# Moving three output-weight blocks of a small MLP to three narrow transfers, and its side table to 128 rows

## The chip, the cores and the metric

One core of a Trainium2 chip runs the whole kernel. The metric is device time in microseconds (us), the median of several executions; for the kernel before it is 706.14 us in 3 runs (705.8 to 706.69).

## What is computed

A decode step of one token for 8 sequences: `x` (8 x 512) is normalised, goes through grouped-query attention over a cache of 4096 positions (8 key/value heads of 128, 32 query heads), and beside that through a gated MLP; the attention output is scaled by the SiLU of the MLP's output and added to `x`. All data is float32.

```
xn = layernorm(x)
q  = xn @ wq ; o = softmax(q k^T / sqrt(128)) v ; s = o @ wo
z  = gelu(xn @ w_in)                 # 8 x 1792
z1, z2 = z[:896], layernorm(z[896:])
y  = (z1 * (w_sp * z2 + b_sp)) @ w_out   # w_out: 896 x 512
out = x + s * silu(y)
```

The key and value caches are 134 MB each, `wq` and `wo` 8.4 MB each, `w_in` 3.7 MB, `w_out` 1.8 MB: seven blocks of 128 rows by 512 columns, 256 KB each.

## The kernel before

**Loads.** A ring of three slots (`slot()`, 128 x 16384 floats, 8 MB each) takes all big loads, issued by SyncE in program order: the MLP weights (`w_mlp`, L64), `wq` (L78), then for each of 8 heads two halves of K (`load_k`, L302) and two of V (`load_v`, L309), at last `wo` in seven pieces (L326). A load into a slot that was used before waits, on SyncE, until the last reader of the slot is done; what stands behind it in SyncE's queue waits too. The fourth load, K's second half of head 0, takes the slot of the MLP weights. The fifth, V's first half, takes that of `wq`, which the query projection reads (`project_q`, L223).

**The small loads** go out on ScalarE's queue: `x` (L57), the side table (L59: 128 rows of 130 floats, with `x` in the final layout and the two scalars `w_sp` and `b_sp`), and `w_low` (L66).

**How a transfer is cut.** Six of the seven blocks of `w_out` (`MAIN`) are part of `w_mlp`, 128 rows with one piece of each row for every partition. Block 1 (`LOW`) is a transfer of its own: its outermost count is 4 (`LOW_E`), within it 4 rows (`LOW_R`); each of these 16 rows (`QR`) holds 8 pieces (`CH`) of 512 floats, so the block lies on 16 partitions as 8 chunks one beside the other. The side table's outermost count is 2 (`SIDE_E`), with 64 rows each. On the host, 64 floats of padding behind each outermost piece keep the outermost count apart from the rest.

**The MLP** (`mlp()`). `xn` is transposed, 32 matmuls over `w_in` (L148) give `z` on four groups of 32 partitions (a group of 32 columns of the PE array each), VectorE and ScalarE work out GELU and the normalisation (L152 to L178), then the scale and shift with the two scalars from the side table (L179) and the product with `z1` (L181). The product is transposed: two transposes of 128 columns (L184) and a copy (L185), and 8 of 16 columns (L191) with 8 copies (L195). Then come the output matmuls into `pw`: six of 128 rows for the whole blocks (L199) and 8 of 16 rows for block 1's chunks (L205). Block j goes to column group j // 2, so block 1's chunks share one group. A float32 matmul appears in the trace as two instructions. The copy of `pw` (L207), the sum over groups (L210) and the SiLU (L212 to L216) follow, then the query projection and the loop over heads.

**A head.** Scores of both K halves (L246), softmax with transposes (L251 to L279), and for each sequence the values (L289) with masking and sum on VectorE (L292, L294) and a small matmul (L298). The end is the product with `wo` (L340, L349) and the gate (L359, L360).

Of the kernel before, what the change touches and what calls it, by code (L numbers as in the profile page):

```python
# [8 lines left out]
F32 = mybir.dt.float32  # L9
# [4 lines left out]
P = 128  # L14
B, D = 8, 512
# [4 lines left out]
R = 32  # L20
# [7 lines left out]
SLOT = HALF * UNIT  # L28
WO_PIECES = [(0, 8), (8, 16), (16, 24), (24, 28), (28, 30), (30, 31), (31, 32)]
FOLDED = 16  # L30
LOW_E, LOW_R = 4, 4
QR = LOW_E * LOW_R
CH = -(-P // QR)
MAIN = [0, 2, 4, 6, 3, 5]
LOW = [1]
SIDE_E = 2
SIDE_N = P // SIDE_E * (P + 2)
N_LOW = len(LOW) * CH * D


@with_exitstack
def tile_gqa_gmlp_decode(ctx: ExitStack, tc: tile.TileContext, x, side, kT, v, wq, wo,
                         w_mlp, w_low, out):
    nc = tc.nc
    const = ctx.enter_context(tc.tile_pool(name="const", bufs=1))
    ring = ctx.enter_context(tc.tile_pool(name="ring", bufs=3))
    work = ctx.enter_context(tc.tile_pool(name="work", bufs=1))
# [4 lines left out]
    def slot():  # L52
        return ring.tile([P, SLOT], F32, name="slot")
# [2 lines left out]
    x_sb = const.tile([B, D], F32, name="x_sb")  # L56
    nc.scalar.dma_start(x_sb, x)  # L57
    side_sb = const.tile([P, P + 2], F32, name="side_sb")
    nc.scalar.dma_start(side_sb, side[:, :SIDE_N].rearrange("e (p n) -> e p n", n=P + 2))  # L59

    mlp_slot = slot()
    n_in, n_mlp = NK * 2 * FH, NK * 2 * FH + len(MAIN) * D
    n_low = n_mlp + N_LOW
    nc.sync.dma_start(mlp_slot[:, :n_mlp], w_mlp)  # L64
    w_in_sb = mlp_slot[:, :n_in].rearrange("p (k n) -> p k n", k=NK)
    nc.scalar.dma_start(mlp_slot[:QR, n_mlp:n_low],  # L66
                        w_low[:, :LOW_R * N_LOW].rearrange("e (i n) -> e i n", n=N_LOW))
    w_out_sb = mlp_slot[:, n_in:n_mlp].rearrange("p (j d) -> p j d", d=D)
    w_low_sb = mlp_slot[:QR, n_mlp:n_low].rearrange("p (j a d) -> p j a d", a=CH, d=D)
    spare = [n_low]  # L70

    def from_slot(rows, n):
        lo = spare[0]
        spare[0] = lo + n
        return mlp_slot[:rows, lo:lo + n]

    wq_sb = slot()
    nc.sync.dma_start(wq_sb, wq)  # L78
# [3 lines left out]
    ident = const.tile([P, P], F32, name="ident")  # L82
# [20 lines left out]
    sc = ps_fix.tile([P, 2, 512], F32, name="sc")  # L103
# [5 lines left out]
    def scratch(shape, name):  # L109
        t = ps.tile([P, 512], F32, name="scr")  # L110
        n = 1
        for s in shape[1:]:
            n *= s
        return t[:shape[0], :n]
# [2 lines left out]
    st = small.tile([B, 6], F32, name="st")  # L117
    mv = small.tile([B, 2], F32, name="mv")
    rstd = small.tile([B, 2], F32, name="rstd")
    xn = from_slot(B, D)  # L120
    nc.vector.bn_stats(st, x_sb)
    nc.vector.bn_aggr(mv, st)
    nc.vector.tensor_scalar(rstd[:, 0:1], mv[:, 1:2], EPS, None, op0=ALU.add)
# [9 lines left out]
    def mlp():  # L133
        zu = work.tile([P, 4, FQ], F32, name="zu", tag="p")
        z, u = zu[:, :2], zu[:, 2:]
        hy = work.tile([P, 2 * D], F32, name="hy", tag="pT")
        hy2 = from_slot(P, CH * P).rearrange("p (a s) -> p a s", a=CH)
        hT = hy[:, :2 * P].rearrange("p (a s) -> p a s", a=2)
        hL = hy2[:QR]
        y_sb, e = zu[:, :2].rearrange("p a f -> p (a f)"), zu[:, 2, :P]  # L140
        pz = scratch([P, 2 * FQ], "pz")
        nc.vector.memset(pz, 0.0)
        for part in range(2):
            for k in range(NK):
                for g in range(G):
                    lo = g * FQ
                    n = min(FQ, FH - lo)
                    nc.tensor.matmul(pz[R * g:R * (g + 1), part * FQ:part * FQ + n], xnT[:, k, :],  # L148
                                     w_in_sb[:, k, part * FH + lo:part * FH + lo + n],
                                     start=(k == 0), stop=(k == NK - 1))  # L150
        zf, uf = z.rearrange("p a f -> p (a f)"), u.rearrange("p a f -> p (a f)")
        nc.vector.tensor_copy(zf, pz)  # L152
        nc.vector.tensor_mul(uf, zf, zf)
        nc.vector.tensor_scalar(uf, uf, 0.044715, 1.0, op0=ALU.mult, op1=ALU.add)
        nc.vector.tensor_mul(uf, uf, zf)
        nc.scalar.activation(uf, uf, AF.Tanh, scale=GELU_C)
        nc.vector.tensor_scalar(uf, uf, 1.0, 0.5, op0=ALU.add, op1=ALU.mult)
        nc.vector.tensor_mul(zf, uf, zf)

        def mean(src, name):  # L160
            part_sum = small.tile([P, 1], F32, name="part_sum")
            nc.vector.tensor_reduce(part_sum, src, op=ALU.add, axis=AX.X)
            pm = scratch([P, 1], "pm")
            nc.tensor.matmul(pm, same_all, part_sum, start=True, stop=True)
            t = small.tile([P, 1], F32, name=name)
            nc.vector.tensor_scalar(t, pm, 1.0 / FH, None, op0=ALU.mult)
            return t

        z1, z2 = z[:, 0, :], z[:, 1, :]
        mu = mean(z2, "mu")  # L170
        nc.vector.tensor_scalar(z2, z2, mu, None, op0=ALU.subtract)
        nc.vector.tensor_mul(u[:, 0, :], z2, z2)
        nc.vector.memset(u[(G - 1) * R:, 0, FH - (G - 1) * FQ:], 0.0)
        var = mean(u[:, 0, :], "var")
        nc.vector.tensor_scalar(var, var, EPS, None, op0=ALU.add)
        rs = small.tile([P, 1], F32, name="rs")
        nc.gpsimd.tensor_tensor(rs, var, neg_half, op=ALU.pow)
        nc.vector.tensor_scalar(z2, z2, rs, None, op0=ALU.mult)  # L178
        nc.vector.tensor_scalar(z2, z2, side_sb[:, P:P + 1], side_sb[:, P + 1:P + 2],  # L179
                                op0=ALU.mult, op1=ALU.add)  # L180
        nc.vector.tensor_mul(u[:, 1, :], z2, z1)  # L181
        th = scratch([P, 2 * P], "th")
        for a in range(2):
            nc.tensor.transpose(th[:, a * P:(a + 1) * P], u[:, 1, a * P:(a + 1) * P], ident)  # L184
        nc.vector.tensor_copy(hT.rearrange("p a s -> p (a s)"), th)  # L185
        for lo in range(0, CH, 4):
            n = min(4, CH - lo)
            tl = scratch([QR, n * P], "tl")
            for a in range(lo, lo + n):
                k = min(QR, P - a * QR)  # L190
                nc.tensor.transpose(tl[:k, (a - lo) * P:(a - lo + 1) * P],  # L191
                                    u[:, 1, P + a * QR:P + a * QR + k], ident)
            for a in range(lo, lo + n):
                k = min(QR, P - a * QR)
                nc.vector.tensor_copy(hL[:k, a], tl[:k, (a - lo) * P:(a - lo + 1) * P])  # L195
        pw = scratch([P, D], "pw")
        for i, j in enumerate(MAIN):
            g, a = divmod(j, 2)
            nc.tensor.matmul(pw[R * g:R * (g + 1), :], hT[:, a, R * g:R * (g + 1)], w_out_sb[:, i, :],  # L199
                             start=(a == 0), stop=(j in (3, 5, 6)))  # L200
        for a in range(CH):
            k = min(QR, P - a * QR)
            for i, j in enumerate(LOW):
                g = j // 2
                nc.tensor.matmul(pw[R * g:R * (g + 1), :], hL[:k, a, R * g:R * (g + 1)],  # L205
                                 w_low_sb[:k, i, a, :], start=False, stop=(a == CH - 1))
        nc.vector.tensor_copy(y_sb, pw)  # L207
        py = scratch([P, P], "py")
        for g in range(G):
            nc.tensor.matmul(py[R * g:R * (g + 1), :], same[:, 0, :], y_sb[:, g * P:(g + 1) * P],  # L210
                             start=True, stop=True)
        nc.vector.tensor_scalar(e, py, -1.0, 87.0, op0=ALU.mult, op1=ALU.min)  # L212
        nc.scalar.activation(e, e, AF.Exp)
        nc.vector.tensor_scalar(e, e, 1.0, None, op0=ALU.add)
        nc.vector.reciprocal(e, e)
        nc.vector.tensor_mul(gate, py, e)  # L216
# [88 lines left out]
    def load_v(h, half, parts):  # L305
# [4 lines left out]
        return t.rearrange("p (i j e) -> p i j e", i=HALF, j=J)  # L310

    mlp()
    project_q(0)
    project_q(1)
    for h in range(HKV):
        for half in range(2):
            scores(h, half, load_k(h, half))
        pT = softmax(h)
# [19 lines left out]
    for m in range(FOLDED):  # L338
        h, r = divmod(m, REP)
        nc.tensor.matmul(part[R * r:R * r + B, :], oT[:, h, r, :], wo_sb[:, m, :],  # L340
                         start=(m < REP), stop=(m >= FOLDED - REP))
# [11 lines left out]
    for g in range(G):  # L353
        nc.tensor.matmul(acc[R * g:R * g + B, :], same[:, 0, :B], part_sb[:, g * P:(g + 1) * P],
                         start=False, stop=False)
# [47 lines left out]
```

## Time and profile before

| what | value |
|---|---|
| median of 3 runs | 706.14 us |
| the profiled execution | 707.1 us |
| its span | 705.3 us |
| mean granted TensorE clock | 0.751 of full speed |
| PE / VectorE busy | 381.4 us (54%) / 174.9 us (25%) |
| bytes moved by DMA | 291.23 MB, 413 GB/s over the span |
| share of DMA in the chain of waits that ended last | 73% |

The profile shows one execution. Its span runs from the first to the last instruction; times within it are us from its start. "Busy" counts an engine's own work, not its waits. PEclk is the clock that TensorE was granted, 1.0 being full speed. PE is the matmul side of TensorE and PEld its weight loads; each matmul instruction has a weight load ahead of it. In the rows of the timeline the columns are start, duration, engine, line, operation, output and input, count, and in brackets how long the engine was idle before and what ended that. In the table of stretches each engine has its busy time and, in brackets, the count of instructions; then come the granted clock, the DMA share and GB/s.

### The profile page before, as it was taken

The numbers are of one execution on the slowest core, as the hardware profiler recorded it, in microseconds if no ns is written. First come the engines' busy times: TensorE is split into PE (matmuls) and PEld (weight loads), VectorE is DVE, ScalarE is ACT, GpSimd is POOL, SyncE is SP. The second block draws the span as 40 slices with busy tenths as digits, with TensorE's granted clock in tenths as the row PEclk, the third lists the DMA queues.
The fourth block names the chain that finished last, engine by engine and source line by source line (L and its number), as shares of the span: only waits on it lengthen the run. The fifth ranks groups of instructions, "written<-read, shape, count | busy, mean of one in ns | idle before, by whom it ended". The sixth has DMA issues, their size and how long they took to land.

```text
span 705.3 us, 5853 instructions
## 1 busy us (share of the span) xinstructions
PE 381.4 (54%) x2630; PEld 118.5 (17%) x2630; DVE 174.9 (25%) x378; ACT 13.5 (2%) x27; POOL 3.7 (1%) x11
## 2 busy tenths in 40 slices
PE   0307875454566456544645557554645466645576
PEld 0202222111211112110211112110211121111223
DVE  2301313230234004310234014300334023400450
ACT  0000000000000000000000000000000000000000
POOL 1000000000000000000000000000000000000000
PEclk9855796776777877877677766876777677787788
DMA  9990799999999999999999999999999999999996
GB/s 414 417 413 26 298 469 417 420 443 439 427 421 455 416 436 446 421 427 439 439 417 446 436 427 425 442 436 424 432 439 439 420 439 435 432 416 443 410 426 248
DMA packets 6670, 291.23 MB, mean 413 GB/s; under 512 B 734, under 2 KB 990, under 8 KB 1382
## 3 DMA queue, kind: packets, MB, share of 16 engines
q1 hardware_dynamic: 6480, 290.52, 95.8%
q8 instruction: 20, 0.33, 0.2%
q10 hardware_dynamic: 166, 0.35, 0.2%
q14 instruction: 4, 0.03, 0.0%
HBM read 290.80 MB, written 0.07 MB: 412 GB/s over the span
## 4 chain that ended last, share of the span: by engine, by line
DMA 73%; PE 17%; issue 4%; another core or an unknown queue 3%; DVE 1%; SPq 0%; POOLq 0%; POOL 0%; DVEq 0%
DMA slot<-in_kT 35%; DMA slot<-in_v 32%; PE sc L246 6%; DMA slot<-in_wo 6%; PE o_ps L289 6%; PE scr L205 2%; PE scr L223 1%; PE sc L349 1%; PE po_ps L298 0%; DVE o_sb L294 0%; PE scr L199 0%; DMA x_sb<-in_x 0%; DVE o_all L292 0%; DVE slot L195 0%
## 5 line engine op out<-in xcount | busy, mean ns | idle before, releaser
L246 PE MATMUL sc<-slot,qz 128*32 128x512 f32 x1024 | 143.3, 723 | 123.3 <-DMA slot<-in_kT 123.3
L289 PE MATMUL o_ps<-slot,pT 128*16 128x512 f32 x1024 | 151.3, 731 | 78.7 <-DMA slot<-in_v 78.7
L292 DVE TENSOR_TENSOR o_all<-o_ps,diag 128x512 f32<-128x512 f32 x64 | 44.3, 692 | 152.8 <-PE o_ps L289 152.7
L251 DVE TENSOR_REDUCE nm<-sc 128x1 f32<-128x1024 f32 x8 | 9.8, 1225 | 263.2 <-PE sc L246 263.2
L246 PEld LDWEIGHTS sc<-slot,qz 128*32 128x32 f32 x1024 | 35.1, 130 | 225.0 <-DMA slot<-in_kT 131.1
L294 DVE TENSOR_REDUCE o_sb<-o_all 128x128 f32<-128x512 f32 x64 | 67.9, 1061 | 2.2
L289 PEld LDWEIGHTS o_ps<-slot,pT 128*16 128x16 f32 x1024 | 29.5, 111 | 158.3 <-issue 107.5
L298 PE MATMUL po_ps<-fold,o_sb 128*128 128x4 f32 x128 | 24.9, 264 | 28.2 <-DVE o_sb L294 28.1
L298 PEld LDWEIGHTS po_ps<-fold,o_sb 128*128 128x128 f32 x128 | 19.2, 189 | 73.4 <-DVE o_sb L294 73.4
L277 PE MATMUL scr<-ident,p 128*128 128x128 f32 x64 | 14.8, 410 | 10.7 <-DVE p L272 10.7
L253 ACT ACTIVATE p<-sc,nm 128x1024 f32<-128x1024 f32 x8 | 8.9, 1114 | 564.3 <-DVE nm L251 564.3
L279 DVE COPY pT<-scr 128x128 f32<-128x128 f32 x64 | 13.9, 284 | 9.5 <-PE scr L277 9.5
L184 PE MATMUL scr<-ident,zu 128*128 128x128 f32 x2 | 0.7, 448 | 26.6 <-DVE zu L181 26.6
L277 PEld LDWEIGHTS scr<-ident,p 128*128 128x128 f32 x64 | 11.8, 213 | 11.1 <-issue 11.1
L148 PE MATMUL scr<-slot,xnT 128*32 128x256 f32 (+1 forms) x64 | 5.4, 475 | 11.7 <-DMA slot<-in_w_mlp 11.7
L205 PE MATMUL scr<-slot 16*32 16x512 f32 x16 | 11.4, 887 | 0.0
L223 PE MATMUL scr<-slot,xnT 128*32 128x512 f32 x64 | 9.0, 717 | 0.0
L256 PE MATMUL scr<-ident,nm 128*1 128x128 f32 x8 | 2.2, 270 | 10.8 <-DVE nm L251 10.8
L349 PE MATMUL sc<-slot,oT 128*8 128x128 f32 x128 | 5.4, 337 | 3.1 <-DMA slot<-in_wo 3.1
L269 PE MATMUL scr<-wl,same 128*128 128x1 f32 x16 | 3.6, 297 | 6.2 <-DVE wl L267 6.2
L179 DVE TENSOR_SCALAR zu<-zu,side_sb 128x256 f32<-128x256 f32 x1 | 0.4, 413 | 24.2 <-DMA side_sb<-in_side 24.2
L272 DVE TENSOR_SCALAR p<-p,w 128x1024 f32<-128x1024 f32 x8 | 6.0, 753 | 0.3
(86 smaller groups left out, 81.4 us busy)
## 6 DMA issues: line engine op xcount, KB each, us to landing
slot<-in_v SPq DMA_DIRECT2D x4, 2048.0 KB, 42.7
slot<-in_wo SPq DMA_DIRECT2D x3, 2048.0 KB, 40.4
slot<-in_w_mlp SPq DMA_DIRECT2D x1, 5120.0 KB, 17.0
slot<-in_wo SPq DMA_DIRECT2D x1, 1024.0 KB
slot<-in_wo SPq DMA_DIRECT2D x1, 512.0 KB, 33.6
slot<-in_wo SPq DMA_DIRECT2D x2, 256.0 KB, 27.0
slot<-in_kT SPq DMA_DIRECT2D x16, 49.0
slot<-in_w_low ACTq DMA_DIRECT2D x1, 256.0 KB
```

Of the source, the lines that this page charges most:

```text
L205: nc.tensor.matmul(pw[R * g:R * (g + 1), :], hL[:k, a, R * g:R * (g + 1)], w_low_sb[:k, i, a, :], start=False, stop=(a == CH - 1))
L223: nc.tensor.matmul(pq[R * g:R * (g + 1), :], xnT[:, k, :], wq_sb[:, k, lo:lo + REP * DH], start=(k == 0), stop=(k == NK - 1))
L246: nc.tensor.matmul(sc[R * g:R * (g + 1), c, :], qz[:, h, b * R:(b + 1) * R], k_sb[:, i, c, g, :], start=(b == 0), stop=(b == B - 1))
L251: nc.vector.tensor_reduce(m, sc, op=ALU.max, axis=AX.XY, negate=True)
L253: nc.scalar.activation(p.rearrange("p j s -> p (j s)"), sc.rearrange("p c s -> p (c s)"), AF.Exp, bias=m, accum_out=l[:, h:h + 1])
L277: nc.tensor.transpose(t[:, j * P:(j + 1) * P], p[:, 4 * c + j, :], ident)
L279: nc.vector.tensor_copy(pT[:, 4 * c + j].rearrange("p b (g r) -> p g b r", g=G), t[:, j * P:(j + 1) * P].rearrange("p (g b r) -> p g b r", ...
L289: nc.tensor.matmul(of[R * c:R * c + G * REP, :], pT[:, j, b, :], v_unit[:, j], start=(j < G), stop=(j >= J - G))
L292: nc.vector.tensor_mul(o_all, o, diag[:, :, None].to_broadcast([P, G, DH]))
L294: nc.vector.tensor_reduce(o_sb, o_all.rearrange("p g d -> p d g"), op=ALU.add, axis=AX.X)
L298: nc.tensor.matmul(po[:, b * REP:(b + 1) * REP], o_sb, fold, start=True, stop=True)
L349: nc.tensor.matmul(acc[R * g:R * g + B, :], oT[:, h, r, :], wo_sb[:, m, g * P:(g + 1) * P], start=(m == FOLDED), stop=(m == HKV * REP - 1))
```

## The change

- `MAIN` shrinks from six whole blocks to four (0, 2, 4, 6). Blocks 1, 3 and 5 go into three transfers, now on SyncE's queue between `w_mlp` and `wq`, all in groups of 4 rows: one of outermost count 8 (6 chunks of 32 rows: block 1 and the second half of block 5, 384 KB), one of 4 (8 chunks of 16 rows: block 3, 256 KB), one of 2 (8 chunks of 8 rows: the first half of block 5, 128 KB). The last lies on partitions 32 to 39, the others start at partition 0.
- The side table is loaded with 128 rows as the outermost count, without padding.
- `xn` and the transposed chunks no longer lie in the slot: `xn` shares a work buffer, the chunks use 512 columns of `hy`.
- The chunks run in batches of at most four: up to four transposes, one copy, up to four matmuls, six batches in all (4, 2, 4, 4, 4, 4). `pw` now is half of the bank pair `sc`, and the two scratch banks serve the transposes.

On PE the order is: the transpose for the whole blocks, the transposes of the first batch, the four whole blocks, the first batch's matmuls, then the transposes of batches two and three, matmuls of batch two, transposes of batch four, matmuls of batch three, and so on: a batch's transposes stand one batch ahead of its matmuls.

```diff
-LOW_E, LOW_R = 4, 4
-MAIN = [0, 2, 4, 6, 3, 5]
-LOW = [1]
+MAIN = [0, 2, 4, 6]
+LOW_R = 4
+def rows_of(j, lo, hi, n):
+    return [(j, r) for r in range(lo, hi, n)]
+LOW = [(8, 0, 0, rows_of(1, 0, P, 32) + rows_of(5, P // 2, P, 32)),
+       (4, 0, 6 * D, rows_of(3, 0, P, 16)), (2, R, 6 * D, rows_of(5, 0, P // 2, 8))]
+LAST = [(1, 96), (3, 112), (5, 56)]
...
-    nc.scalar.dma_start(side_sb, side[:, :SIDE_N].rearrange("e (p n) -> e p n", n=P + 2))
+    nc.scalar.dma_start(side_sb, side)
...
-    nc.scalar.dma_start(mlp_slot[:QR, n_mlp:n_low],
-                        w_low[:, :LOW_R * N_LOW].rearrange("e (i n) -> e i n", n=N_LOW))
+    for (e, p0, c0, chunks), w_low in zip(LOW, lows):
+        t = mlp_slot[p0:p0 + e * LOW_R, n_mlp + c0:n_mlp + c0 + len(chunks) * D]
+        nc.sync.dma_start(t, w_low[:, :LOW_R * len(chunks) * D].rearrange("e (i n) -> e i n", i=LOW_R))
+        low_sb.append(t.rearrange("p (c d) -> p c d", d=D))
...
-    xn = from_slot(B, D)
+    xn = work.tile([B, D], F32, name="xn", tag="pT")
...
-        hT = hy[:, :2 * P].rearrange("p (a s) -> p a s", a=2)
-        hL = hy2[:QR]
+        hT, hL = hy[:, :P], hy[:, P:].rearrange("p (a s) -> p a s", s=P)
...
+        th = scratch([P, P], "th")
+        nc.tensor.transpose(th, u[:, 1, :P], ident)
+        nc.vector.tensor_copy(hT, th)
+        pw = sc[:, 0, :]
         for i, j in enumerate(MAIN):
+            g = j // 2
+            nc.tensor.matmul(pw[R * g:R * (g + 1), :], hT[:, R * g:R * (g + 1)], w_out_sb[:, i, :],
+                             start=True, stop=(j == 6))
+        for (ne, p0, _, chunks), w_low in zip(LOW, low_sb):
+            n = ne * LOW_R
+            for lo in range(0, len(chunks), 4):
+                some = chunks[lo:lo + 4]
+                tl = scratch([n, len(some) * P], "tl")
+                for i, (j, r) in enumerate(some):
+                    nc.tensor.transpose(tl[:, i * P:(i + 1) * P], u[:, 1, P + r:P + r + n], ident)
+                nc.vector.tensor_copy(hL[p0:p0 + n, :len(some)].rearrange("p a s -> p (a s)"), tl)
+                for i, (j, r) in enumerate(some):
+                    g = j // 2
+                    nc.tensor.matmul(pw[R * g:R * (g + 1), :], hL[p0:p0 + n, i, R * g:R * (g + 1)],
+                                     w_low[:, lo + i, :], start=False, stop=((j, r) in LAST))
```

## The prediction

> **What bounds the kernel now.** I began with the page's slices (17.6 us each) and then asked the trace for long stretches.
>
> ```profile
> span 705.3 us, 5853 instructions
> DMA  9990799999999999999999999999999999999996
> GB/s 414 417 413 26 298 469 417 420 443 439 427 421 455 416 436 446 421 427 439 439 417 446 436 427 425 442 436 424 432 439 439 420 439 435 432 416 443 410 426 248
> ```
>
> ```profile
> core 0: us, PE busy (x) PEld busy (x) DVE busy (x) ACT busy (x) POOL busy (x), PEclk, DMA share, GB/s
> 0.00:53.00 53.00, 7.06 (x72) 4.54 (x72) 10.11 (x29) 1.91 (x2) 3.73 (x11) 0.77 0.99 414
> 58.00:75.00 17.00, 16.52 (x38) 4.09 (x38) 2.49 (x10) 0.00 (x0) 0.00 (x0) 0.60 0.01 3
> 97.00:650.00 553.00, 305.74 (x2048) 91.25 (x2052) 133.11 (x231) 9.86 (x21) 0.00 (x0) 0.74 1.00 433
> ```
>
> From 97 to 650 us the transfers run at share 1.00 and 433 GB/s: this part lasts as long as its bytes. There is one hole, from 58 to 75 us, with 3 GB/s. Whatever ends the hole earlier or later moves everything behind it by as much, so I looked for what ends it, in SyncE's queue and in the chain of waits.
>
> ```profile
> 74.66 0.33 SPq L302 DMA_DIRECT2D slot<-in_kT  x1
> ...
> 86.36 8.80 SPq L309 DMA_DIRECT2D slot<-in_v  x2
> ```
>
> ```profile
> SPq L302 <- DMA slot<-in_w_low: 56.4, 1, 56.4
> ...
> SPq L302 <- PE scr L205: 15.2, 1, 15.2
> ```
>
> ```profile
> 0.74 2.47 DMA x_sb<-in_x
> ...
> 32.46 0.35 DVE zu L178
> 32.82 24.14 another core or an unknown queue
> ...
> 57.05 0.42 DVE zu L179
> ...
> 57.50 0.43 DVE zu L181
> ...
> 57.98 0.69 PE scr L184 x2
> 58.67 0.87 PE scr L191 x4
> ...
> 60.48 2.83 PE scr L199 x12
> 63.32 11.32 PE scr L205 x16
> ```
>
> ```profile
> DVE zu L179 <- DMA side_sb<-in_side: 24.2, 1, 24.2
> ```
>
> The second half of K needs the slot that holds the MLP weights. SyncE issues it at 74.66, as the last matmul that reads that slot (L205) ends; call this moment M, 74.64 us now. MLP had waited 24.2 us for the side table, then took 16.7 us. So M is set by: w_mlp landed, arithmetic, side table, output matmuls. The forecast is a forecast of M.
>
> **The change part by part.**
>
> *Side table.* I read the outermost count of a transfer, capped at 16, as the number of streams it runs on; so 16 streams of 8 rows take the place of two of 64. Now it lands at about 57 us, having been issued ahead of the big loads; a row seems to get through between rows of the big loads.
>
> ```profile
> 1.36 0.62 ACTq L59 DMA_DIRECT2D side_sb<-in_side  x1
> ```
>
> If 64 rows in turn took 57.0 − 2.0 = 55 us, a row took at most 0.86 us on average. Eight rows then give 2.0 + 8 × 0.86 = 8.9 us. As some may have gone in a bunch at the end, my upper bound is 8 rows that each wait for a 64 KB row at 433/16 = 27 GB/s, 2.4 us: 21 us. Both lie ahead of 31 us, when it is first wanted (below). So this wait of 24.2 us goes. What is late next is the PE. The Trainium skill (DMA: Bandwidth & Descriptors, "Why a DMA increments its semaphore by 16 and not by 1") has a transfer run on as many engines, up to 16, as divide its outermost counts: by that 2 before and 16 after. No view here shows single engines.
>
> *w_mlp.* Issued at 0.74, landed 17.0 us later:
>
> ```profile
> slot<-in_w_mlp SPq DMA_DIRECT2D x1, 5120.0 KB, 17.0
> slot<-in_w_low ACTq DMA_DIRECT2D x1, 256.0 KB
> ```
>
> It loses two blocks of six, 512 KB, 1.3 us at 414 GB/s. w_low leaves ScalarE's queue, where it ran beside w_mlp: 64 KB on each of four streams, 2.5 us at 414/16 = 26 GB/s if those streams were last, 0 if not. I take the middle, 1.3. Together 2.6 us earlier, bounds 1.3 and 3.8. The three new transfers (768 KB) stand behind w_mlp on SyncE's queue; their heaviest streams carry 48 + 64 + 64 = 176 KB, 6.8 us, so they land by about 22 us, far ahead of 31. wq and K's first half are pushed back by as much at most, into the hole: nothing, while M stays above some 61 us (the old end of the transfers, 55 to 56 us in the slices, less 1.3, plus 6.8). The added issues cost SyncE under a microsecond each and it has nothing else to do.
>
> *From w_mlp to the gated product.*
>
> ```profile
> 17.91 5.36 PE L148 MATMUL scr<-slot,xnT 128*32 128x256 f32 x64 [11.70 <-DMA slot<-in_w_mlp]
> ```
>
> From 17.91 to the end of L178 (32.81) is 14.9 us, L179 and L181 with their gaps 0.95: without the side wait the first transpose would start at 33.8, with w_mlp 2.6 us earlier at **31.2**. L148 depends on when the clock rises under it: between about 5.1 us and, all at half clock, 6.9. Bounds of this start: 29.7 and 34.0.
>
> *Output matmuls.* L205 is 8 matmuls (two instructions each) on one column group, one after the other. Now 22 chunks (6 of 32 rows, 8 of 16, 8 of 8) follow four whole blocks. The price of one depends on the granted clock. These are the weight loads, one per instruction at L205, four at L223, which uses four column groups at once:
>
> ```profile
> 64.56 0.10 PEld L205 LDWEIGHTS scr<-slot 16*32 16x32 f32 x1 [0.32 <-issue]
> 64.99 0.10 PEld L205 LDWEIGHTS scr<-slot 16*32 16x32 f32 x1 [0.32 <-issue]
> ...
> 66.74 0.17 PEld L205 LDWEIGHTS scr<-slot 16*32 16x32 f32 x1 [0.68 <-issue]
> 67.60 0.17 PEld L205 LDWEIGHTS scr<-slot 16*32 16x32 f32 x1 [0.68 <-issue]
> ...
> 77.55 0.20 PEld L223 LDWEIGHTS scr<-slot,xnT 128*32 128x32 f32 x4 [0.66 <-issue]
> 78.40 0.20 PEld L223 LDWEIGHTS scr<-slot,xnT 128*32 128x32 f32 x4 [0.66 <-issue]
> ```
>
> 0.43 us an instruction early in L205, 0.855 later, and 0.855 for one with 128 rows too: the rows do not change the price, the clock does. 22 chunks × 2 × 0.855 = 37.6 us at half clock, 18.9 at full. Which of them holds I read in windows of 3.41 us, the step in which the clock changes:
>
> ```profile
> 59.30:62.71 3.41, 3.30 (x16) 0.98 (x15) 1.73 (x8) 0.00 (x0) 0.00 (x0) 0.55 0.02 5
> 62.71:66.12 3.41, 3.41 (x11) 0.83 (x8) 0.00 (x0) 0.00 (x0) 0.00 (x0) 0.95 0.00 0
> 66.12:69.53 3.41, 3.41 (x5) 0.69 (x4) 0.00 (x0) 0.00 (x0) 0.00 (x0) 0.50 0.00 0
> 69.53:72.95 3.42, 3.42 (x5) 0.69 (x4) 0.00 (x0) 0.00 (x0) 0.00 (x0) 0.50 0.00 0
> ...
> 76.36:79.78 3.42, 3.42 (x20) 0.79 (x16) 1.54 (x4) 0.31 (x1) 0.00 (x0) 0.55 0.71 307
> 79.78:83.19 3.41, 2.58 (x28) 0.90 (x24) 1.12 (x8) 0.00 (x0) 0.00 (x0) 1.00 0.71 308
> ```
>
> ```profile
> 154.87:158.28 3.41, 2.20 (x12) 0.60 (x16) 0.00 (x0) 0.00 (x0) 0.00 (x0) 0.50 0.84 365
> 158.29:161.70 3.41, 3.41 (x20) 0.79 (x16) 0.00 (x0) 0.00 (x0) 0.00 (x0) 0.55 1.24 538
> ```
>
> After a window full of 128-row matmuls or transposes (59.30, 76.36) the clock is 1.0; 2.20 us of them (154.87) did not raise it. L205, 16 rows on one column group, filled 62.71 to 66.12 nearly alone: the clock fell, and three more windows of it left it at 0.5. The new chunks use at most 32 rows of 128, also one group, so I take half clock throughout, **37.6 us**; full clock is the other bound.
>
> Ahead of them: one transpose and four of the first batch (0.22 each by L191, some 0.3 until visible) 1.4, then four blocks on four column groups, two rounds of 0.855: 3.2 us with the hand-over. The chunks come in six batches of at most four through one buffer: transposes, a copy, matmuls. A copy of batch n+1 into the same partitions waits for the matmuls of batch n, while PE has the next transposes queued. The copy:
>
> ```profile
> 74.66 0.69 DVE L207 COPY zu<-scr 128x512 f32<-128x512 f32 x1 [13.38 <-PE scr L205]
> ```
>
> So between batches stand 0.2 us drain, 0.69 copy and some 0.1 of semaphores, beside four transposes of 0.87: about 1.05 us. At the first change, six transposes and a shorter copy, 1.45. Five changes: 1.45 + 4 × 1.05 = 5.6 us (bounds 4.4, all hidden but the copies, and 7). With a last drain of 0.2: 3.2 + 37.6 + 5.6 + 0.2 = **46.6 us**, where 16.7 stood.
>
> **Sum:** M = 31.2 + 46.6 = 77.8 us, 3.2 later than 74.64. Behind M all is as before: q projection, V at M + 11.7, while K's half is still landing. Span 705.3 + 3.2 = 708.5. The profiled execution took 707.1, 1.8 more than its span, and lies 1.0 above the median of the runs, 706.14; on the median: 706.14 + 3.2 = **709.3 us**. In one line: 24.2 of waiting and 2.6 of loading are gained, and 46.6 − 16.7 = 29.9 of serial work is paid.
>
> **The rivals.**
>
> *A: the chunks run at full clock* (not slower). It decides in the first window full of chunks, at about 36 us. Half clock for the first 5 us, then 42 instructions × 0.43 + five changes of 0.9 + 0.2 = 22.8: M = 31.2 + 27.9 = 59.1, 15.5 us earlier, about 690.6 us. The two streams with the extra 176 KB drain by 61 and K's start then is at 60.4, so at most 0.6 is lost again. For it: 32 rows are twice L205's 16. Against: in the window from 66.12 PE was busy for 3.41 of 3.41 us at 0.50. The Trainium skill (TensorE: Matmul & The Clock Gate, Part 1) says that a busy window of 3.4 us releases the clock and only idle ones throttle it; by that rule A comes true, and the quoted windows disagree with it. Chance 10%.
>
> *B: one or two windows at full clock.* Transposes and whole blocks fill 1.4 + 1.7 = 3.1 us; where a window falls on them as at 59.30, the next has full clock and saves 3.4 us: M = 74.4, 705.9 us, no change; two windows make 702.5. For it: L199 was so raised. Against: 2.20 us of work raised nothing, and three in four positions of the window cut the 3.1 us. Chance 20%, a quarter of it for two windows.
>
> *C: the side table still comes with the end of the big loads.* M = 57.98 + 46.6 = 104.6, 30 us later: 736. Against it: x, one row a stream on the same queue, landed at 0.74 + 2.47 = 3.21. Chance 4%.
>
> **How the numbers follow.** Forecast 66%, A 10%, B 20%, C 4%. The forecast's own range: start 29.7 to 34.0 and changes 4.4 to 7 give M from 75.1 to 82.0, mostly 76.4 to 80: 707.9 to 711.5. The range for 8 in 10 takes in B with two windows: **702 to 711.8**. About 0.2% (1.4 us) is what a measurement can tell from no change. Slower: 0.62 of the forecast, C, a little of B: 0.68. Same: most of B with one window and a bit of the forecast: 0.15. Faster: A, two windows and early starts of B: 0.17.
>
> **What would show it.** Side table: no wait for it at the scale and shift, which run at about 30 us. Early w_mlp: the first MLP matmul between 14 and 17 us. Serial chunks: their weight loads 0.855 us apart at clock 0.50, with five gaps of about 1 us; some 46 us from the first transpose to the last chunk. M: the issue of K's second half at about 78 us and a DMA hole from about 61 to 78, everything behind shifted by 3 us. The forecast is wrong if loads stand 0.43 us apart (A), if K's second half goes out before 74 us, or if 97 to 650 us no longer runs at 433 GB/s.

## The result and the profile after

| | before | after |
|---|---|---|
| median | 705.97 us (705.56 to 706.69, 4 runs) | 710.49 us (709.67 to 710.74, 4 runs) |
| the profiled execution / its span | 707.1 / 705.3 us | 710.74 / 708.9 us |
| M, last read of the MLP slot | 74.64 us | 78.29 us |
| mean granted clock | 0.751 | 0.735 |

The ratio is 1.0061 (95% interval 1.0043 to 1.0078): slower by 4.5 us, where 3.2 were forecast (709.3 us).

From the page of the changed kernel, its span and the two rows of slices for DMA (17.7 us each):

```profile
span 708.9 us, 5936 instructions
DMA  9990599999999999999999999999999999999996
GB/s 386 447 404 26 237 415 463 418 423 459 415 429 453 411 436 451 411 440 445 414 441 437 425 433 441 429 430 437 433 426 437 441 422 430 444 423 429 412 427 255
```

The hole in the fourth slice is still there, and the fifth slice is emptier (237 GB/s, 298 before). The stretches of the changed kernel, in the same columns as before, and what SyncE's queue waited for with K's second half:

```profile
61.00:79.00 18.00, 16.51 (x22) 2.77 (x20) 1.36 (x2) 0.00 (x0) 0.00 (x0) 0.50 0.00 0
100.00:653.00 553.00, 309.11 (x2028) 91.22 (x2032) 133.03 (x231) 9.85 (x21) 0.00 (x0) 0.73 1.00 432
```

```profile
SPq L293 <- PE sc L196: 57.5, 1, 57.5
```

Behind the hole the transfers run as before, share 1.00 and 432 GB/s; nothing was lost or won there. The chain of waits in between (start, duration, what):

```profile
30.33 0.37 DVE zu L174
30.70 0.03 issue
30.72 0.42 DVE zu L175
...
31.65 0.47 PE scr L179
32.13 0.85 PE scr L192 x4
32.98 1.87 PE sc L184 x8
34.85 6.96 PE sc L196 x8
41.81 1.39 PE scr L192 x6
43.20 3.55 PE sc L196 x4
46.75 0.95 PE scr L192 x4
...
70.51 0.69 DVE hy L193
71.20 0.04 issue
71.25 7.04 PE sc L196 x8
78.29 0.02 issue
```

L175, the scale and shift with the side table, follows L174 by 0.03 us: the wait of 24.2 us is gone. In its place stands one almost unbroken block of PE from 31.65 to 78.29 (its one gap, 0.8 us, lies ahead of the last batch): six batches, with the transposes of the next but one batch between them.

### The profile page after: what moved, and what is told of

Read it like the earlier page. It is cut to its first block, busy times and chain, and to the rows that moved or that the text cites. A ratio compares the mean times of both kernels' runs of the same rounds, so it can differ in the third digit from the quotient of the medians.

```text
span 708.9 us, 5936 instructions
## 1 busy us (share of the span) xinstructions
PE 417.8 (59%) x2667; PEld 124.1 (18%) x2667; DVE 176.7 (25%) x376; ACT 13.5 (2%) x27; POOL 3.7 (1%) x11
## 4 chain that ended last, share of the span: by engine, by line
DMA 72%; PE 22%; issue 4%; DVE 1%; SPq 0%; POOLq 0%; POOL 0%
DMA slot<-in_kT 34%; DMA slot<-in_v 32%; PE sc L237 7%; PE o_ps L280 6%; DMA slot<-in_wo 6%; PE sc L196 5%; PE scr L214 1%; PE sc L340 1%; PE scr L192 1%; PE po_ps L289 0%; DVE o_sb L285 0%; PE sc L184 0%; DMA x_sb<-in_x 0%; DVE o_all L283 0%; SPq L317 0%
## 5 line engine op out<-in xcount | busy, mean ns | idle before, releaser
L237 PE MATMUL sc<-slot,qz 128*32 128x512 f32 x1024 | 148.8, 746 | 122.6 <-DMA slot<-in_kT 122.6
L196 PE MATMUL sc<-slot,hy 16*32 16x512 f32 (+2 forms) x44 | 38.8, 1056 | 0.8 <-DVE hy L193 0.8
L193 DVE COPY hy<-scr 16x512 f32<-16x512 f32 (+3 forms) x6 | 3.8, 635 | 34.9 <-PE sc L196 25.4
L144 PE MATMUL scr<-slot,xnT 128*32 128x256 f32 (+1 forms) x64 | 6.5, 549 | 9.3 <-DMA slot<-in_w_mlp 9.3
L196 PEld LDWEIGHTS sc<-slot,hy 16*32 16x32 f32 (+2 forms) x44 | 6.6, 163 | 27.7 <-issue 23.9
L331 PE MATMUL sc<-slot,oT 128*8 128x512 f32 x32 | 6.0, 878 | 1.3 <-DMA slot<-in_wo 1.3
```

The source lines that it names most:

```text
L196: nc.tensor.matmul(pw[R * g:R * (g + 1), :], hL[p0:p0 + n, i, R * g:R * (g + 1)], w_low[:, lo + i, :], start=False, stop=((j, r) in LAST))
L237: nc.tensor.matmul(sc[R * g:R * (g + 1), c, :], qz[:, h, b * R:(b + 1) * R], k_sb[:, i, c, g, :], start=(b == 0), stop=(b == B - 1))
```

## The experiments

M in each is the time in the trace at which the last output matmul ends. The kernel before ran beside each set: 702.42 to 706.74 us beside the first four, 706.54 beside the next four, 702.21 to 707.16 beside the last three.

**The side table alone.** The kernel before, with only its side table changed:

```diff
-    nc.scalar.dma_start(side_sb, side[:, :SIDE_N].rearrange("e (p n) -> e p n", n=P + 2))
+    nc.scalar.dma_start(side_sb, side)
```

> The kernel before with one change, the side table in 128 rows; output weights as before (six whole blocks, block 1 in 8 chunks). My theory (M, the last read of the MLP slot, moves everything 1:1 until the DMA hole is closed): the wait of 24.2 us for the side table goes, M is about 50 us, before the transfers run dry at 55 us; the hole of 20 us closes and the time is 686 us (684.5 to 688). Rival 1 (the side table's wait is not what counts, the narrow transfers are): no change, 706 us. Rival 2 (more rows in the queue slow the big loads as much as is gained): 700 us or more.

Measured: 684.54 us (684.52 to 684.55), ratio 0.9713 (0.9676 to 0.9749); M = 49.13. The chain, and the page's DMA rows:

```profile
31.15 0.37 DVE zu L178
31.52 0.03 issue
31.54 0.42 DVE zu L179
...
37.91 11.22 PE scr L205 x16
49.13 0.02 issue
```

```profile
DMA  9999999999999999999999999999999999999996
GB/s 373 445 446 439 430 431 434 427 434 430 427 431 434 435 434 438 435 427 430 443 434 431 426 438 431 430 435 434 431 434 431 434 427 430 427 434 427 419 428 258
```

The slice with 26 GB/s is gone. This one line is worth about 20 us (18 to 22, by the scatter of the kernel before); both rivals fall. So in the changed kernel the other half, the chunks, gave all of that back and more.

**All blocks whole.** As the experiment above, and in addition `MAIN = [0, 2, 4, 6, 1, 3, 5]` in `w_mlp`, with no narrow transfer, no chunks and no `w_low`.

> The side table in 128 rows and all seven w_out blocks whole in w_mlp, no narrow transfer and no chunks. My theory: M is about 38 us, but the hole is closed already by 55 us, so it gains nothing over the kernel with the side table alone except what the four heavier streams cost there: 685.5 us (684 to 687), 0 to 2 us below that one. Rival (each us of M still counts): 12 us below that one, about 674 us.

Measured: 684.96 us (684.68 to 685.06), M = 37.40: seven blocks take 3.67 us.

```profile
33.73 3.67 PE scr L176 x14
37.40 0.02 issue
37.42 38.52 DMA slot<-in_kT
```

M is 11.7 us earlier than with the side table alone and the time is the same to 0.4 us (above it, where 0 to 2 us below were expected). The rival (each us of M counts) falls: below 49 us M counts no longer.

**Neighbouring chunks on different column groups.** In the changed kernel, only the list of rows is another; `LAST` follows it.

```diff
-LOW = [(8, 0, 0, rows_of(1, 0, P, 32) + rows_of(5, P // 2, P, 32)),
-       (4, 0, 6 * D, rows_of(3, 0, P, 16)), (2, R, 6 * D, rows_of(5, 0, P // 2, 8))]
+LOW = [(8, 0, 0, [(1, 64), (3, 64), (5, 64), (1, 96), (3, 96), (5, 96)]),
+       (4, 0, 6 * D, [(j, r) for r in range(0, P // 2, 16) for j in (1, 3)]),
+       (2, R, 6 * D, rows_of(5, 0, P // 2, 8))]
```

> The changed kernel with other rows of blocks 1, 3 and 5 in the same three transfers, so that neighbouring chunks of the first two transfers lie on different column groups; number of chunks, batches, bytes and waits unchanged. My theory (the 37.6 us come from matmuls that share one column group): batches one to four take 10.3 us in place of 24, M is 12 us earlier, 66 us, and the time 698.5 us (697 to 700). Rival (each matmul costs 0.855 us wherever it lies, for instance because fewer than 128 rows don't run side by side): no change, 710.5 us.

Measured: 695.42 us (694.81 to 696.17), ratio 0.9868 (0.9836 to 0.99) to the kernel before; M = 63.67, 14.6 us earlier than in the changed kernel, time 15.1 lower. The chain:

```profile
34.87 3.55 PE sc L197 x8
38.41 1.39 PE scr L193 x6
39.81 1.85 PE sc L197 x4
...
47.11 7.80 PE sc L197 x16
```

The first batch takes 3.55 us where it took 6.96, with as many instructions and the same loads: up to three groups work at a time (the second batch, on two groups, took 1.85 us for 3.55). The time came out 1.6 us below my range: the fifth batch (one group) ran beside the fourth (two others), 16 instructions in 7.80 us, which I had not counted. The rival (no overlap) falls. The clock did not rise with the groups; the window of the first batch:

```profile
34.41:37.82 3.41, 3.41 (x12) 0.54 (x8) 0.00 (x0) 0.00 (x0) 0.00 (x0) 0.50 1.15 500
```

**The side table back in two groups**, in the changed kernel:

```diff
-    nc.scalar.dma_start(side_sb, side)
+    nc.scalar.dma_start(side_sb, side[:, :SIDE_N].rearrange("e (p n) -> e p n", n=P + 2))
```

> The changed kernel with the side table again in 2 groups of 64 rows, the rest unchanged. My theory: the table comes with the end of the big loads on the two heaviest streams, at about 61 us, M is about 109 us and the time 741 us (735 to 745). Rival (it is not the number of rows per stream that held the table, but the narrow transfer behind it on ScalarE's queue): no change, 710.5 us.

Measured: 741.54 us (one run); the table was waited for 32.0 us, L177 came at 61.57, M was 109.1.

```profile
DVE zu L177 <- DMA side_sb<-in_side: 32.0, 1, 32.0
```

As my theory had it; the rival falls, since no narrow transfer stands behind the table on ScalarE's queue here. With the first experiment this measures the one line in both kernels: about 20 us in the kernel before (where the end of the transfers caps it), 31 in the changed one (741.54 − 710.49).

**128 rows in place of 8 to 32.** Each chunk matmul is replaced by one with all 128 rows of a whole block of its column group, so the MLP's output is another.

```diff
-                    nc.tensor.matmul(pw[R * g:R * (g + 1), :], hL[p0:p0 + n, i, R * g:R * (g + 1)],
-                                     w_low[:, lo + i, :], start=False, stop=((j, r) in LAST))
+                    nc.tensor.matmul(pw[R * g:R * (g + 1), :], hT[:, R * g:R * (g + 1)],
+                                     w_out_sb[:, g, :], start=False, stop=((j, r) in LAST))
```

> The changed kernel with each of the 22 chunk matmuls replaced by one of 128 rows (the whole block of the same column group again), still one column group at a time, so the MLP's output is not the reference's; transposes, copies and loads stay. Theory R (what counts for the granted clock is the rows in use: 128 rows keep PE counted as busy): the clock is 1.0 from the second window on, weight loads stand 0.43 us apart, M is about 59 us and the time 691.5 us (690 to 694). Theory G (it is the column groups in use, one of four is too little): clock 0.50, 0.855 us apart, M 77 to 78 us, 709 to 711 us.

Measured: 686.75 us (one run). The windows of 3.41 us, first of the changed kernel, then of this one (PE, PEld, DVE, ACT, POOL, granted clock, DMA share, GB/s):

```profile
34.41:37.82 3.41, 3.41 (x8) 0.70 (x5) 0.00 (x0) 0.00 (x0) 0.00 (x0) 0.50 1.15 500
37.82:41.23 3.41, 3.41 (x5) 0.52 (x3) 0.00 (x0) 0.00 (x0) 0.00 (x0) 0.50 0.98 423
71.92:75.33 3.41, 3.41 (x5) 0.69 (x4) 0.00 (x0) 0.00 (x0) 0.00 (x0) 0.50 0.00 0
```

```profile
34.41:37.82 3.41, 3.41 (x8) 0.80 (x6) 0.00 (x0) 0.00 (x0) 0.00 (x0) 0.77 1.13 485
37.82:41.23 3.41, 3.41 (x13) 0.89 (x12) 0.50 (x2) 0.00 (x0) 0.00 (x0) 1.00 0.99 423
48.05:51.46 3.41, 3.41 (x11) 0.89 (x8) 0.00 (x0) 0.00 (x0) 0.00 (x0) 1.00 0.75 327
```

PE is busy for the whole of every window shown; the clock is 0.50 with few rows and 1.00 with 128, on one column group in both. Theory G falls, here and by the mixed order, where two and three groups stayed at 0.50; R holds. Whether it is the rows as such or the number of PE cells at work (128 x 32 here, at most 3 x 32 x 32 in the mixed order) was not separated. The time came out below R's range, since no copy waits for matmuls here (they no longer read the copied chunks), so that only transposes stand between the batches and M came at 53.9 us, not 59.

**Filling the other groups.** Beside each chunk three more matmuls of 128 rows, in the other column groups, into the idle half of `sc`; their result is not used.

```diff
+                    for f in range(G):
+                        if f != g:
+                            nc.tensor.matmul(sc[R * f:R * (f + 1), 1, :], hT[:, R * f:R * (f + 1)],
+                                             w_out_sb[:, f, :], start=True, stop=True)
```

> The changed kernel with three more matmuls of 128 rows beside each chunk, one in each other column group, into an idle half of the bank pair (66 more matmuls; the result is not used). If the work in the other groups runs beside the chunks and raises the clock: 1.0 from the second window on, M about 59 us in spite of four times the work, time about 691.5 us (690 to 695). If it runs beside them and the clock stays: M 78, 710 us. If matmuls of 32 rows and of 128 rows cannot run side by side: each chunk takes about twice as long at full clock, M some 75 to 85 us, 707 to 717 us.

Measured: 752.34 us (one run), outside all three. Timeline:

```profile
37.20 1.91 PE L196 MATMUL sc<-slot,hy 32*32 32x512 f32 x2
39.04 1.93 PE L200 MATMUL sc<-slot,hy 128*32 128x512 f32 x6
40.90 1.91 PE L196 MATMUL sc<-slot,hy 32*32 32x512 f32 x2
```

A chunk, then its three companions, then the next chunk, 1.85 us each: the chunks do not run beside matmuls of 128 rows even on other column groups, while the three of 128 rows run beside each other. That the companions write into another bank is not the reason: in the kernel before, into one bank, the first chunk (16 rows, column group 0) also waited for the last two whole blocks (groups 1 and 2), though its own group was free from about 62.2 us:

```profile
62.20 0.18 PEld L199 LDWEIGHTS scr<-slot,hy 128*32 128x32 f32 x2 [0.67 <-issue]
63.24 0.13 PEld L205 LDWEIGHTS scr<-slot 16*32 16x32 f32 x2 [0.86 <-issue]
```

A window of the run with filled groups:

```profile
37.82:41.23 3.41, 3.41 (x9) 0.37 (x8) 0.00 (x0) 0.00 (x0) 0.00 (x0) 0.50 0.91 389
```

The clock stayed at 0.50, with about half of the window on 128 rows. So the third expectation had the order right, one after the other, but not the clock, and with it the time. As a way to raise the clock this failed.

**Without 8, without 16 of the chunks.** The loop over the transfers is cut to `LOW[:2]` and `LOW[:1]`; the transfers stay, the work on the left-out chunks goes (and with it part of the MLP's output).

> The changed kernel without the work on the 8 chunks of 8 rows (first half of block 5; transposes, copies and matmuls left out, the transfer stays), so the MLP's output is not the reference's. My theory: two batches less, 2 x (6.84 + 1.05) = 15.8 us, M is 62.5 us, just behind the end of the first transfers, and the time follows 1:1: 694.7 us (693.5 to 696). Rival (the hole shrinks but the heaviest streams, 176 KB more, set a floor above that): 698 us or more.

Measured: 695.26 us (one run), 15.2 less than the changed kernel; M = 62.5, 15.8 less. Time follows M nearly 1:1 down to there.

> The changed kernel without the work on blocks 3 and the first half of 5 (16 chunks left out, all transfers stay), so the MLP's output is not the reference's. M is about 46.7 us, ahead of the end of the first transfers (55 us on most streams, 59 us on the two heaviest), and the hole is closed. If each stream works off its own bytes and all later loads are cut evenly, the two heaviest streams, 127 KB more than in the kernel with whole blocks, end 4.7 us later than there: 685.0 + 4.7 = 689.7 us (688.5 to 691). Rival (the uneven loads cost nothing, since another stream ends last anyway): 685 us (684 to 686.5).

Measured: 685.72 us (one run), M = 45.6; 0.8 above the kernel with whole blocks. My figure for the uneven loads, 4.7 us, was wrong, the rival right in size: the narrow transfers, by the prediction's count 128 KB more on two streams than whole blocks put there (176 against 48), cost less than 1 us. No view shows single streams, so that count itself is not shown, and why so little is lost stays open.

**The kernel before, twice more.** Its times had fallen into two groups, 702 to 703 and 706 to 707 us.

> The kernel before, unchanged, another look. On the chip of the first experiments its times fell into two groups, 702.4 to 703.2 and 706.3 to 706.7 us, 3.5 us apart, the step of the clock's windows (3.41 us). Theory W (where the free windows of the clock fall on the output matmuls decides whether one more window of them runs at full clock): in a run near 703 us L205 has about 6.8 us at 1.0 and M is about 71 us; in one near 706.5 us it has 3.4 us or less, M 74 to 75 us. Rival (the two groups come from the transfers): M is 74 to 75 us in both, and the difference shows behind 97 us.

> As the look before it: theory W ties the time to M, time = 706.1 + (M - 74.6); the rival leaves M at 74 to 75 us whatever the time is.

Measured: 703.25 and 705.84 us. The chains of the first and of the second:

```profile
57.86 0.69 PE scr L184 x2
...
62.82 8.33 PE scr L205 x16
71.15 0.02 issue
```

```profile
56.80 0.69 PE scr L184 x2
...
62.03 11.43 PE scr L205 x16
73.46 0.02 issue
```

M = 71.15 and 73.46; 706.1 + (M − 74.6) gives 702.7 and 705.0, 0.6 and 0.8 below what was measured. That formula joins the M of one execution to the median of others; with that execution's own time, 707.1 + (M − 74.64), it gives 703.6 and 705.9, within 0.4. L205 took 8.33 us where the clock was 1.0 for two windows (61.5 to 68.4 us), 11.43 with one (61.0 to 64.4). The rival falls, since M moved, and theory W holds for these two executions, one of each group: the one near 703 us caught a window more at full clock. Why its second window stayed at 1.0 is not shown; L199, with 128 rows, had reached 1.3 us into the window before it, against 1.0 us in the other run. This is the effect that the prediction named as B, at work in the kernel before.

**The changed kernel again.**

> The changed kernel, unchanged, once more beside the kernel before on one chip, since the experiments ran on another chip than the first comparison. My theory: its chunks never raise the clock, so its times form one group, 709.5 to 711 us, whatever group the kernel before falls into there; against a kernel before of 703 us the ratio is 1.010, against 706.4 us it is 1.006. Rival (the chip itself is faster, and both kernels with it): 706 to 708 us.

Measured: 710.34 us (709.36 to 710.85, 7 runs) beside a kernel before of 706.34 (702.21 to 707.16, 10 runs); ratio 1.0067 (1.0044 to 1.0089). One group, as expected; its M was 77.66.

## Why the prediction was right, point by point

- *M decides.* Right. M moved by 3.65 us, the span by 3.6; three experiments with M at 62.5, 63.7 and 109.1 us moved the time by as much (within 0.6 us). In every profiled execution with M from 53.9 to 109.1 us the time is M + 632 to 633 us, which meets the 685 us of those with M at 37.4 and 49.1 at 52 to 53 us: there M stops to count. The prediction had that limit at some 61 us, and the hole starting there, by the load of its two heaviest streams. In the changed kernel the transfers thin out well before (DMA share 0.53, then 0.09), and the last rows land by 57 us. So that limit was wrong; it changed nothing here, because M lay above both.

```profile
51.46:54.87 3.41, 3.41 (x6) 0.54 (x5) 0.17 (x1) 0.00 (x0) 0.00 (x0) 0.50 0.53 231
54.87:58.28 3.41, 3.41 (x8) 0.84 (x7) 1.19 (x2) 0.00 (x0) 0.00 (x0) 0.50 0.09 38
```

- *The side table's wait goes.* Right, shown alone in both kernels. The table landed 17.8 us after its issue at 1.3, so at 19.1: far from the estimate of 8.9, near the upper bound of 21, and still ahead of 30.7, when it was wanted.
- *w_mlp earlier.* The size was off a little: the first MLP matmul came at 14.67 in place of 17.91, 3.2 us, where 2.6 were taken from bounds of 1.3 and 3.8. L144 gave back 1.1 of it: 6.46 us, nearly all at half clock, in place of 5.36. The first transpose came at 31.65, forecast 31.2: two misses that partly cancel.

```profile
14.67 6.46 PE L144 MATMUL scr<-slot,xnT 128*32 128x256 f32 x64 [9.32 <-DMA slot<-in_w_mlp]
```

- *Output matmuls at half clock, in series.* Right: 78.29 − 31.65 = 46.64 us, forecast 46.6. So close a match is luck in part: the work ahead of the chunks took 3.2 us as forecast, but the six batches took 38.4 (forecast 37.6; each is 0.1 to 0.2 us longer than its instructions at 0.855, about what the prediction took as drain), and the five changes 5.0 (forecast 5.6, and 0.2 for the last drain). Weight loads 0.855 us apart at clock 0.50:

```profile
72.11 0.17 PEld L196 LDWEIGHTS sc<-slot,hy 8*32 8x32 f32 x1 [0.68 <-issue]
72.96 0.17 PEld L196 LDWEIGHTS sc<-slot,hy 8*32 8x32 f32 x1 [0.68 <-issue]
```

  That they lie on one column group and that few rows leave the clock at half both cost much: the mixed order took 14.6 us off M, the run with 128 rows 24.4, part of it because no copy is waited for there. The two were not run together, so whether they add up is not shown.
- *Rivals.* A fell in the changed kernel; in the run with 128 rows the clock rose. By the Trainium skill (TensorE: Matmul & The Clock Gate, Part 1) a busy window of some 3.4 us brings the full clock; here some 46 us of busy PE stayed at 0.50, so with matmuls of 32 rows and less that did not hold. B did not happen in the profiled runs of the changed kernel. C did not happen; with the table back in two groups it does.
- *The median.* The span came out 0.4 above the forecast, the median 1.2. The 0.4 is M. For the rest: the M of 74.64 us belongs to an execution of 707.1 us, and I had put the difference on the median of 706.14, 1.0 below it. With its own time the step is exact, 707.1 + 3.65 = 710.75, where the profiled execution of the changed kernel took 710.74. The kernel before scatters by a window of clock (3.4 us) from run to run, the changed one by 1.5 us.

The best of all these kernels is the one with only the side table changed, 684.54 us, 0.9713 of the kernel before; whole blocks throughout are equal to it within 0.4 us and have the shorter code.

## What to carry to other kernels

Where transfers fill the time, look for the one place where they stop, find the last wait ahead of it, and change nothing else: a small table held up 20 us here, and the rest of the change cost 26 (710.49 − 684.54). Cutting weights into pieces of few rows to fit narrow transfers multiplies matmuls whose price does not fall with the rows; put neighbours on different column groups, or leave the blocks whole. And a gain ahead of such a place counts only until the next limit (here 52 to 53 us), so compute where it stops before paying for more.

## What the runs showed of the hardware that was not expected

- A matmul of 32 rows or less and one of 128 rows did not overlap on different column groups (1.85 us each in turn at clock 0.50), while matmuls of 32 rows among themselves did (4 instructions on two groups in 1.85 us, on one in 3.55), and so did three of 128 rows.
- PE busy for 3.41 of 3.41 us did not raise the clock above 0.50 with matmuls of 8 to 32 rows, on one column group or on up to three; matmuls of 128 rows on one group raised it to 1.00.
- The kernel before runs at about 703 or 706.5 us; in the two executions looked at, one more window of 3.41 us at full clock fell on eight matmuls in the faster one.
- The three narrow transfers in place of whole blocks cost 0.8 us, not the 4.7 that 128 KB more on two streams would take.
